# Backward 32x32 products on eight tiles of TensorE, in two PSUM banks, with a new order of heads

## The chip, the cores and the metric

One core of one Trainium2 chip runs the whole program: TensorE (PE, with its weight loads as PEld), VectorE (DVE), ScalarE (ACT), GpSimd (POOL) and the queue of SyncE (SP), from which most transfers are issued. The metric is the device time of one execution in microseconds (us). A measurement is the median of several runs; the profile is one more execution, taken by the hardware profiler.

## What is computed

A forward pass and the gradients of all its inputs, in bf16. Sequence 2048, width 512, 32 heads of 128, 64 segments of 32 rows, and 8 memory rows that go from each segment to the next. Cut to what matters:

```python
for s in range(n_seg):                       # 64, one after the other
    h = concatenate([mem, x_s])              # 8 + 32 rows
    q, k, v = (einsum('td,dhe->hte', h, W) for W in (Wq, Wk, Wv))
    p = softmax(where(mask, q @ k.T * scale, -1e9))
    o = einsum('hte,hed->td', p @ v, Wo)
    mem = o[:M]; outs.append(o[M:])
out = x + attention(layernorm(x)) + mlp(layernorm(x))     # mlp: relu(.)**2
grads = vjp(out)(grad_out)                   # x, mem0, Wq, Wk, Wv, Wo, w1, b1, w2, b2
```

The backward runs through the segments from the last to the first; the gradient of a segment's 8 memory rows is added to the output gradient of the segment before it. For each head it needs dP = gO v', dS from dP and P, and then dV = P'gO, dK = dS'q, dQ = dS k: products that contract over 32 rows and give 32 rows of 128.

## The kernel before

It has four stages: the MLP with its own backward, the forward recurrence, the backward recurrence, and the weight gradients with the layernorm backward.

**Layout.** The 32 heads of a segment stand as [128, 8, 128]: partition 32j + r holds row r of one head of group j (j = 0 to 3), and i = 0 to 7 counts the heads of the group. Head number is 4i + j. Memory rows of four segments (a block) form one more such array, the L arrays.

**Order.** In the first three stages nothing is ordered by hand. Each operation is added to a `_Plan` (L40) with a cost, the keys that it reads and writes, and a priority; `_Plan.run` (L101) lists them by the longest path that hangs on each, places each on its engine by its own estimate, and emits all engines' instructions in that order. `_TURN` (L22) is what the plan charges for a change of the shape of TensorE's tiles: "d" (32x32), "w" (128x32) and "f" (full array). A PSUM bank is a key too: `Stage.bank` (L350) deals the banks of a kind out in turn when an operation is added, before the plan is made.

**Backward recurrence** (`chain`, L1300, once a segment): project the output gradient (ps_gO, `proj`, L415), evict to gN, transpose on TensorE (ps_gOT), product dP (L1313), softmax gradient on VectorE (L1165 to L1170) into dS (the tile maskA), two 32x32 transposes of it on VectorE. Then three parts (L1319) for t = 2, 1, 0, each: products by `diag` (L441) in two halves into ps_d, eviction to dN, 32x32 transposes on VectorE (`sq_T`, L395) to dT, and four groups of matmuls against the transposed weights (`dh_part`, L1174) that add up in ps_dRA. That is copied to R_A, the memory rows are taken from it by small matmuls (ps_gm), and a copy puts them into the gradient of the segment before (L1353).

**32x32 products.** `diag` puts the matmul of group j on the tile at (32j, 32j): four of the array's sixteen tiles. A half is four of the eight i in one bank, two terms each (rows of the segment, and its memory rows):

```python
nc.tensor.matmul(
    bk()[32 * j:32 * j + m, k * P:(k + 1) * P], lhsT=lf(j, i), rhs=rf(j, i),
    start=(k == 0 and x == 0), stop=(x == n - 1), tile_position=(32 * j, 32 * j),
    skip_group_check=True,
)
```

**Block work.** `l_pre` (L1192) and `l_post` (L1228) do the same for the L arrays once per four segments, with lower priority: gL, gLT, dPL, dqL (by `diag`), then dL (an own part on 32x32 tiles at L1258, and a part over four segments read back from memory, L1269), and ps_dRL. They fill TensorE where the chain waits.

**Banks of the backward** (L1155): five of kind c for gO, gOT, dP, the chain's products and gm; one r for ps_dRA; two f for the block work. While the weights are turned (`turn`, L363), `rings` (L1379) deal differently.

**Last stage** (from L1500, ordered by hand): sixteen rounds of 20 x 8 matmuls [128, 512] into all eight banks, evicted in turn by ScalarE and VectorE. The plan before it does the first four banks of six rows of round 0 early (pw0, L1424).

Of the kernel before, what the change touches and what calls it, by code (L numbers as in the profile page):

```python
# [17 lines left out]
P = 128  # L18


_HOP = 0.06
_TURN = 0.095  # L22
# [13 lines left out]
class _Op:  # L36
    __slots__ = ("idx", "cost", "fn", "prio", "deps", "users", "left", "done", "end", "eng", "lat", "shape", "lift")


class _Plan:  # L40
# [12 lines left out]
    def add(self, cost, fn, R=(), W=(), prio=1, lat=None, lift=0.0):  # L53
        o = _Op()
        o.lift = lift
# [7 lines left out]
        o.users = []  # L63
        deps = set()
# [36 lines left out]
    def run(self):  # L101
# [4 lines left out]
        for o in reversed(ops):  # L106
            c = min(o.cost.values())
            t = 0.0
            for u in o.users:
                same = o.cost.keys() == u.cost.keys() and "SP" not in o.cost  # L110
                t = max(t, rank[u.idx] + (0.0 if same else o.lat + _HOP))
            rank[o.idx] = c + t + o.lift
# [3 lines left out]
        seq = []  # L116
        while elig:
            cand = []
            for o in elig:
                best = None  # L120
                g = _HOP + (0.0 if o.prio == 0 else self.grace)
                for e, c in o.cost.items():
                    t = 0.0
                    for d in o.deps:
                        t = max(t, d.end if d.eng == e and e != "SP" else d.end + d.lat + g)
                    s = max(t, free.get(e, 0.0) + (_TURN if o.shape not in (None, shape) else 0.0))
                    if best is None or s + c < best[0]:
                        best = (s + c, s, e, c)
# [32 lines left out]
            o.done = True  # L161
            elig.remove(o)
# [11 lines left out]
class _Bank:  # L174


    def __init__(self, pool, key, shape, dt, name):
        self.pool, self.key, self.shape, self.dt, self.name = pool, key, shape, dt, name
        self.t = None

    def __call__(self):
        if self.t is None:
            self.t = self.pool.tile(self.shape, self.dt, name=self.name, tag="%s%d" % self.key)
        return self.t
# [3 lines left out]
def kernel(  # L188
# [152 lines left out]
    class Stage:  # L341


        def __init__(self, plan, pools):
            self.plan = plan
            self.pools = pools
            self.cnt = {}
            self.rings = {}

        def bank(self, kind, shape, dt, name):  # L350
            ring = self.rings.get(kind) or [(kind, x) for x in range(self.pools[kind][1])]
            key = ring[self.cnt.get(kind, 0) % len(ring)]
            self.cnt[kind] = self.cnt.get(kind, 0) + 1
            return _Bank(self.pools[key[0]][0], key, shape, dt, name)
# [8 lines left out]
        def turn(self, kind, nm, reg, key, okey, g0=0, g1=DC * NI // 2):  # L363

            for g in range(g0, g1):
                dc, i0 = g % DC, 2 * (g // DC)
                blk = reg[:, dc, i0 * JQ * P:(i0 + 2) * JQ * P]
                bk = self.bank(kind, [P, 8, P], BF16, "ps_" + nm)

                def tr(e, blk=blk, bk=bk):  # L370
                    src = blk.rearrange("p (i m c) -> p i c m", i=2, c=JQ)
                    for i in range(2):
                        for c in range(JQ):
                            transpose_to(bk()[:, JQ * i + c, :], src[:, i, c, :])
                self.plan.add(pe(0.46, "f"), tr, [key] if g > g0 else [], [bk.key] + ([] if g > g0 else [key]), 1)
                self.evict(lambda blk=blk: blk, bk,
                           lambda bk=bk: bk()[:].rearrange("p k d -> p (k d)"), [(okey, g)], 1, {"DVE": 0.7, "ACT": 1.0})

        def turn_o(self, kind, nm, reg, key, okey, lift=0.0):

            for g in range(2 * NI):
# [8 lines left out]
                self.plan.add(pe(0.46, "f"), tr, [key] if g else [], [bk.key] + ([] if g else [key]), 1, lift=lift)  # L390
# [12 lines left out]
        def evict(self, out_f, bk, in_f, W, prio, cost, R=()):  # L403
            self.plan.add(cost, lambda e: ev({"DVE": "v", "ACT": "s"}[e], out_f(), in_f()),
                          [bk.key] + list(R), W, prio)

        def proj(self, kind, nm, win, wkeys, Wt, col0, dst, prio):
            for half in range(2):
                bk = self.bank(kind, [P, 512], F32, "ps_" + nm)
                for dq in range(2):  # L410
# [8 lines left out]
                    self.plan.add(pe(0.435, "w"), mm, wkeys, [bk.key], prio)  # L419
# [3 lines left out]
        def to_T(self, kind, nm, src, skeys, out_f, okeys, prio):  # L423
            for half in range(2):
# [5 lines left out]
                self.plan.add(pe(0.225, "f"), tr, [skeys[half]], [bk.key], prio)  # L430
# [3 lines left out]
        def to_T_plain(self, kind, nm, src, sk, dst, dk, prio):  # L434
# [4 lines left out]
                      [(dk, 0), (dk, 1)], prio)  # L439

        def diag(self, kind, nm, terms, rkeys, dst, prio, by=None):  # L441
            n = len(terms)
            for half in range(2):
# [12 lines left out]
                self.plan.add(pe(0.23 * n, "d"), mm, rkeys(half), [bk.key], prio)  # L456
                if by:
# [10 lines left out]
                    self.plan.add({"DVE": 0.70, "ACT": 0.92}, sc, [bk.key, by[0]], [(dst[0], half)], prio)  # L468
# [17 lines left out]
    def wf(t):  # L486
        w = Wqkv[t].rearrange("p c (i j e) -> p c i j e", i=NI, j=JQ)
        return lambda dc, c0: w[:, dc, c0 % HW // P:c0 % HW // P + 4, c0 // HW, :]
# [5 lines left out]
    def wtf(t, h):  # L494
# [28 lines left out]
    with tc.tile_pool(name="p0", bufs=1) as p0, \  # L523
# [41 lines left out]
        sg = Stage(plan, {"h": (pp, 4), "B": (pp, 4)})  # L565
# [12 lines left out]
        def ln(g):  # L578
# [24 lines left out]
            for k in range(2):  # L603
# [3 lines left out]
                A(pe(0.3, "f"), tr, [("xnN", w, k)], [bk.key])  # L607
            A({"DVE": 0.7}, lambda e: V.tensor_copy(xT[g % 2], bk()[:]), [bk.key], [("xT", g % 2)])
# [4 lines left out]
        def mlp_a(g):  # L613
            z = g % 2
            for fc in range(FC):
# [3 lines left out]
                for x, (Wt, wk, In, ik) in enumerate(((W1, ("W1", fc // 8), xT[z], ("xT", z)), (W2T, ("W2T", fc // 2), gTb[z], ("gT", z)))):  # L619
# [4 lines left out]
                    A({"PE": 0.44}, mm, [wk, ik], [bk.key] + ([("tick", g, fc)] if x else []))  # L624
                A({"ACT": 0.36}, lambda e, r=r, fc=fc, bk=bk: nc.scalar.activation(
                    r[:], bk()[:, 0, :], ACT.Relu, bias=b1T[:, fc:fc + 1], scale=1.0), [bk.key, "b1T"], [rk])
# [4 lines left out]
                    accum_out=gb1p[:, fc, g:g + 1]), [bk.key, rk], [("gh", z, fc), ("gb1p", fc, g)])  # L631
# [5 lines left out]
        def mlp_b(g):  # L637
            z, y3 = g % 2, g % 3
            for rc in range(2):
# [5 lines left out]
                A({"PE": 0.22}, b2m, ["b2r"], [bB.key])  # L645
# [924 lines left out]
```

## Time and profile before

| | us |
|---|---|
| median of 3 runs (3017.47 to 3035.89) | 3026.65 |
| span of the profiled execution | 3018.8 |
| TensorE busy | 2761.1 (91%) |
| VectorE busy | 1551.3 (51%) |
| ScalarE busy | 967.4 (32%) |
| forward recurrence, about | 230 to 1240 |
| backward recurrence, about | 1302 to 2440 |
| last stage, about | 2470 to 3019 |

Costliest groups in the backward by line: L1181 (ps_dRA) 382.5 us busy, L399 (sq_T to dT) 255.6, and each of the six terms of L451 on ps_d 67.6 to 74.3 (the six overlap; together L451 is busy 236.9 us from 1302 to 2422).

How to read it: a matmul's row gives its own length, filling and draining included, so that rows of neighbours overlap; the busy time of a group is the union of its rows. "128*32 128x512" is a matmul on 128 rows and 32 columns of the array whose moving operand has 512 columns. The chain of waits is followed back from the last instruction of the span or of a window: at each step to what released it.

### The profile page before, as it was taken

The page shows a single profiled execution, that of the slowest core. Times are in us where ns is not written, and L with a number is a line of the kernel's source. Part 1 is how long each engine was busy: PE and PEld are TensorE (multiplying, and loading weights), DVE is VectorE, ACT ScalarE, POOL GpSimd, SP SyncE. Part 2 cuts the span into 40 slices and gives each one's busy share as a digit, 9 for nine tenths or more (in the row PEclk, how much of TensorE's full clock was granted, in tenths as well). Part 3 has the DMA queues.
Part 4 walks back from the last instruction along what each step waited for, and adds up shares of the span by engine and source line. Part 5 has one row for each costly group of instructions (what it writes and reads, how often), then busy time and mean ns, then how long its engine had stood idle before and what let it go on. Part 6 is the DMA issues. An engine that isn't in the chain of part 4 may idle for free.

```text
span 3018.8 us, 132985 instructions
## 1 busy us (share of the span) xinstructions
PE 2761.1 (91%) x59680; PEld 1575.5 (52%) x59680; DVE 1551.3 (51%) x3367; ACT 967.4 (32%) x2013; POOL 372.8 (12%) x640
## 2 busy tenths in 40 slices
PE   8998899999999999888888888888889889999998
PEld 6664555555555555655454545454555444444444
DVE  5544555555555655666555555565556522232322
ACT  4324444444454444333333333333333310000000
POOL 1111111111111111100000000000000002111111
PEclk9999999999999999899999999999999999999999
DMA  6648655556555666457777877777777689788861
GB/s 202 221 141 227 166 170 168 162 159 172 167 166 162 174 182 179 135 162 197 196 208 197 211 215 208 202 204 207 204 215 205 193 292 311 232 262 271 248 182 42
DMA packets 543946, 590.15 MB, mean 195 GB/s; under 512 B 230342, under 2 KB 344183, under 8 KB 541199
## 3 DMA queue, kind: packets, MB, share of 16 engines
q1 hardware_dynamic: 527934, 527.05, 61.2%
q0 software_dynamic: 15440, 54.61, 5.4%
q8 instruction: 466, 7.63, 1.1%
q14 instruction: 106, 0.86, 0.1%
HBM read 283.32 MB, written 262.68 MB: 181 GB/s over the span
## 4 chain that ended last, share of the span: by engine, by line
PE 64%; issue 11%; DMA 10%; DVE 9%; SPq 2%; ACT 2%; POOL 1%; DVEq 0%; ACTq 0%; POOLq 0%
PE ps_gw L1517 11%; PE ps_dRA L1181 7%; PE ps_d L451 6%; PE ps_q L415 4%; PE ps_k L415 3%; PE ps_RA L863 3%; PE ps_h L622 3%; PE ps_gO L415 3%; PE ps_dw L1073 2%; PE ps_v L415 2%; PE ps_dRL L1181 2%; PE ps_B L650 2%; SPq L361 2%; PE ps_gxb L650 2%; DMA dLN<-S_GNL 1%
## 5 line engine op out<-in xcount | busy, mean ns | idle before, releaser
L1181 PE MATMUL ps_dRA<-WA,dT 128*32 128x512 bf16 x6144 | 382.5, 388 | 13.9 <-issue 10.2
L1517 PE MATMUL ps_gw<-WA,WB 128*128 128x512 bf16 x1536 | 332.3, 379 | 0.6 <-DVE gwo L316 0.6
L415 PEld LDWEIGHTS <-PA 128*32 128x32 bf16 x8192 | 204.9, 98 | 239.2 <-DVE PA L1011 27.0
L399 DVE STREAM_TRANSPOSE dT<-dN 128x512 bf16<-128x512 bf16 x384 | 255.6, 692 | 104.9 <-ACT dN L318 103.4
L1517 PEld LDWEIGHTS <-WB 128*128 128x128 bf16 x1896 | 185.4, 98 | 225.0 <-issue 1.7
L318 ACT CAST dN<-ps_d 128x512 bf16<-128x512 f32 x357 | 199.2, 588 | 287.5 <-PE ps_d L451 270.1
L1181 PEld LDWEIGHTS <-dT 128*32 128x32 bf16 x6144 | 158.5, 98 | 175.7 <-issue 34.4
L316 DVE CAST gwo<-ps_gw 128x512 bf16<-128x512 f32 x64 | 39.7, 683 | 401.7 <-PE ps_gw L1517 268.2
L318 ACT CAST gwo<-ps_gw 128x512 bf16<-128x512 f32 x64 | 32.9, 599 | 515.4 <-PE ps_gw L1517 357.9
L1291 POOL COPY bVT<-VR 128x1024 bf16<-128x1024 bf16 x64 | 66.7, 1043 | 965.9 <-PE ps_dP L1313 917.7
L415 PE MATMUL ps_q<-WA,PA 128*32 128x512 bf16 x2048 | 159.3, 387 | 8.4 <-DVE PA L1011 8.3
L316 DVE CAST kN<-ps_k 128x512 bf16<-128x512 f32 x120 | 83.0, 691 | 160.4 <-PE ps_k L415 158.7
L451 PEld LDWEIGHTS <-PB 32*32 32x32 bf16 x8192 | 119.1, 92 | 79.3 <-issue 45.9
L415 PE MATMUL ps_k<-WA,PA 128*32 128x512 bf16 x2048 | 158.0, 385 | 0.0
L415 PE MATMUL ps_gO<-WB,PA 128*32 128x512 bf16 x2048 | 138.3, 414 | 16.8 <-DVE PA L1353 15.3
L863 PE MATMUL ps_RA<-WB,OT 128*32 128x256 bf16 x4096 | 128.3, 275 | 14.6 <-DVE OT L399 10.5
L318 ACT CAST qN<-ps_q 128x512 bf16<-128x512 f32 x124 | 72.6, 586 | 198.8 <-PE ps_q L415 183.0
L1073 PE MATMUL ps_dw<-sx,anT 128*128 128x512 bf16 x448 | 123.7, 384 | 9.3 <-DMA sx<-in_grad_out_dram 4.7
L415 PE MATMUL ps_v<-WA,PA 128*32 128x512 bf16 x2048 | 129.3, 380 | 0.0
L863 PEld LDWEIGHTS <-OT 128*32 128x32 bf16 x4096 | 103.9, 97 | 39.1 <-DVE OT L399 30.6
L844 POOL TENSOR_TENSOR P<-P,rsA 128x320 bf16<-128x320 bf16 x64 | 46.2, 722 | 534.3 <-DVE rsA L839 228.1
L1181 PE MATMUL ps_dRL<-WA,LT 128*32 128x512 bf16 x1536 | 108.9, 387 | 2.3 <-issue 1.2
(307 smaller groups left out, 4920.1 us busy)
## 6 DMA issues: line engine op xcount, KB each, us to landing
S_GN<-dN SPq DMA_DIRECT2D x192, 256.0 KB
WA<-S_GN SPq DMA_DIRECT2D x160, 256.0 KB
S_Q<-qN SPq DMA_DIRECT2D x64, 256.0 KB
S_K<-kN SPq DMA_DIRECT2D x64, 256.0 KB
S_V<-vN SPq DMA_DIRECT2D x64, 256.0 KB
S_ON<-oN SPq DMA_DIRECT2D x64, 256.0 KB
bqN<-S_Q SPq DMA_DIRECT2D x64, 256.0 KB
bkN<-S_K SPq DMA_DIRECT2D x64, 256.0 KB
```

Of the source, the lines that this page charges most:

```text
L316: nc.vector.tensor_copy(out, in_)
L318: nc.scalar.copy(out, in_)
L399: self.plan.add({"DVE": 0.70}, lambda e, x=x: nc.vector.transpose(dst[:, x, :, :], src[:, x, :].rearrange("p i (a c) -> p i c a", c=JQ)), ...
L415: nc.tensor.matmul(bk()[32 * j:32 * (j + 1), :], lhsT=win(dc), rhs=Wt(dc, c0), start=(dc == 0), stop=(dc == DC - 1), tile_position=(0, 32 ...
L451: nc.tensor.matmul(bk()[32 * j:32 * j + m, k * P:(k + 1) * P], lhsT=lf(j, i), rhs=rf(j, i), start=(k == 0 and x == 0), stop=(x == n - 1), ...
L622: nc.tensor.matmul(bk()[:, x, :], lhsT=Wt[:, dc, fc * P:(fc + 1) * P], rhs=In[:, dc, :], start=(dc == 0), stop=(dc == DC - 1), skip_group_ ...
L650: nc.tensor.matmul(bk()[:], lhsT=src[z][:, fc, rc * P:(rc + 1) * P], rhs=Wt[:, fc, :], start=(fc == 0 and first), stop=(fc == FC - 1))
L863: nc.tensor.matmul(bk()[32 * c:32 * (c + 1), :], lhsT=OTt[:, i, j, :], rhs=Wo[:, JQ * i + j, dh * DH:(dh + 1) * DH], start=(i == 0 and j < ...
L1073: nc.tensor.matmul(bks[x]()[:], lhsT=anT[x][:, c, :], rhs=sx[z][:], start=(c == 0), stop=(c == TC - 1))
L1181: nc.tensor.matmul(bk()[32 * j:32 * (j + 1), :], lhsT=XT[:, i, j, :], rhs=wtf(t, JQ * i + j), start=(first and i == 0), stop=(last and i = ...
L1291: A({"POOL": 1.0}, lambda e: nc.gpsimd.tensor_copy(VT[:, :, :, M:KA].rearrange("p i j r -> p (i j) r"), VR[:].rearrange("p i j r -> p (i j ...
L1517: nc.tensor.matmul(bks[n]()[:], lhsT=HNc[:, rc, dc * P:(dc + 1) * P], rhs=gns[y][:, hf * 512:(hf + 1) * 512], start=(y == 0), stop=(y == N ...
```

## The change

It does three things.

1. **Heads dealt anew.** Head number is now 16 (i // 4) + 4 j + i % 4. The weights of q, k, v keep their place in memory, and the views of them change (`wf`, `wtf`, `turn`, the load of Wo, the writes of out_3 to out_6).
2. **Eight tiles.** In the backward, `cross` takes the place of `diag`. A half takes the groups j = 2 half and 2 half + 1 with all their i. The matmul of (j, i) goes to the tile at (32j, 32c), c = i % 4, so its result is at partition 32c; the two j of a half go to two banks, of which 256 columns each are used. Results stand as if i and j had changed their roles, and so `dh_part` asks `wtf` for another head. The forward's `diag` stays.
3. **Banks from the scheduler.** A `_Bank` of the backward has no key until the plan places its first operation; then it takes the free bank of its kind that came free earliest (`slots`). The kinds: c (at most 3), f (at most 1) and w (at most 3) share three banks, r has one, d two pairs, and t (turning the weights) uses r and the pairs. `l_post`'s own part and its other part follow each other in one pair. Three early banks, not four, serve the last stage, and they wait for gNat.

`ACCP` and `LIFT` are new parameters of the plan; both are zero.

```diff
-        sg = Stage(plan, {"c": (pc, 5), "r": (pc, 1), "f": (pc, 2)})
+        S3 = [("c", x) for x in range(3)]
+        sg = Stage(plan, pc, {"c": (3, S3), "f": (1, S3), "w": (3, S3), "r": (1, [("r", 0)]), "d": (2, [("d", 0), ("d", 1)]),
+                              "t": (3, [("r", 0), ("d", 0), ("d", 1)])})
...
+        def slots(o):
+            got = []
+            for w in o.banks:
+                if w.key is None:
+                    n, ways = w.group.ways[w.kind]
+                    if used.get(w.kind, 0) + sum(x[3].kind == w.kind for x in got) >= n:
+                        return None
+                    taken = [x[2] for x in got]
+                    can = [(loose.get(k, 0.0), x, k, w) for x, k in enumerate(ways)
+                           if loose.get(k, 0.0) is not None and k not in taken]
+                    if not can:
+                        return None
+                    got.append(min(can, key=lambda x: x[:2]))
+            return got
...
+        def cross(self, nm, terms, rkeys, dst, prio, lift=0.0):
+
+            n = len(terms)
+            for half in range(2):
+                bk = self.bank("d", [P, 2, 512], F32, "ps_" + nm)
+
+                def mm(e, half=half, bk=bk):
+                    self.cross_mm(bk, half, terms, True)
+                self.plan.add(pe(0.115 * n, "d"), mm, rkeys(half), [bk, (dst[0], half)], prio, lift=lift)
+                self.cross_evict(half, bk, dst, prio)
+
+        def cross_mm(self, bk, half, terms, first):
+            for s_ in range(2):
+                for x, (lf, rf, m) in enumerate(terms):
+                    for y in range(2):
+                        j = 2 * half + y
+                        for c in range(JQ):
+                            i = JQ * s_ + c
+                            nc.tensor.matmul(
+                                bk()[32 * c:32 * c + m, y, s_ * P:(s_ + 1) * P], lhsT=lf(j, i), rhs=rf(j, i),
+                                start=(first and s_ == 0 and x == 0), stop=(x == len(terms) - 1),
+                                tile_position=(32 * j, 32 * c), skip_group_check=True,
+                            )
+
+        def cross_evict(self, half, bk, dst, prio):
+            self.evict(lambda: dst[1][:, 4 * half:4 * half + 4, :].rearrange("p (y s) e -> p y (s e)", y=2), bk,
+                       lambda: bk()[:, :, 0:2 * P], [(dst[0], half)], prio, EV_F)
...
     def wf(t):
-        w = Wqkv[t].rearrange("p c (i j e) -> p c i j e", i=NI, j=JQ)
-        return lambda dc, c0: w[:, dc, c0 % HW // P:c0 % HW // P + 4, c0 // HW, :]
+        w = Wqkv[t].rearrange("p c (s j f) -> p c s j f", s=2, j=JQ)
+        return lambda dc, c0: w[:, dc, c0 % HW // 512, c0 // HW, :]
...
-    def wtf(t, h):
+    def wtf(t, i, q):
+        h = 16 * (i % 2) + JQ * (i // 2) + q
         return Wqkv[t][:, :, h * P:(h + 1) * P]
...
-                sg.diag("c", "d%d" % t, terms, rk, ("dN%d" % t, dN[t]), 0)
+                sg.cross("d%d" % t, terms, rk, ("dN%d" % t, dN[t]), 0, LIFT[t])
...
-                    A(pe(0.24, "d"), own, lk, [bks[half].key])
+                    A(pe(0.12, "d"), own_mm, lk + rk, [bk, ("dLN", half)])
...
-        pw0 = [sg.bank("c", [P, 512], F32, "ps_gw") for _ in range(4)]
+        pw0 = [sg.bank("w", [P, 512], F32, "ps_gw") for _ in range(3)]
...
-            A(pe(0.87, "f"), mm0, [("gn", y), ("HN", RCS[y] // BPC)], [b.key for b in pw0])
+            A(pe(0.65, "f"), mm0, [("gn", y), ("HN", RCS[y] // BPC), "gNat"], pw0)
...
-                                             rhs=gns[y][:, hf * 512:(hf + 1) * 512],
+                                             rhs=gns[y].rearrange("p (j s e) -> p s j e", j=JQ, s=2)[:, hf],
```

## The prediction

> **What bounds the kernel now.** I read the stages first, then the backward stage by line, then its chain of waits, then single bursts. The busy time by stretch (length, then each engine's busy us with its instruction count, granted TensorE clock, DMA share, GB/s) sets the backward recurrence, 1302 to 2422 us, beside a stretch of the last stage:
>
> ```profile
> 1302.00:2422.00 1120.00, 976.70 (x30197) 567.13 (x30189) 649.24 (x1293) 358.53 (x664) 90.13 (x138) 0.96 0.74 203
> 2500.00:2900.00 400.00, 400.00 (x1855) 181.37 (x1854) 113.94 (x187) 22.59 (x44) 72.66 (x101) 1.00 0.83 260
> ```
>
> The view of tile ps_gm (duration shortest/median/longest in ns, first and last start in us) gives the period:
>
> ```profile
> L1353 DVE CAST PA<-ps_gm x63: 152/192/193, 1301.8 to 2422.3; 128x32 bf16<-128x32 f32 x63
> ```
>
> The copy that hands one segment's memory gradient to the next has 62 periods in 1120.5 us, so a backward segment takes 18.1 us. TensorE is busy for 976.7 of the 1120 (15.8 us of a segment), VectorE for 58%, ScalarE for 32%. TensorE's work bounds the stage, with about 2.3 us of waiting per segment on top. The chain of waits over part of a segment (start, us, what) says where the work stands:
>
> ```profile
> 1845.52 0.33 PE ps_gOT L312 x4
> 1845.85 0.56 PE ps_d L451 x32
> 1846.40 0.34 PE ps_gOT L312 x4
> ...
> 1847.11 0.70 DVE dT L399
> 1847.81 0.47 DVE btA L1165
> 1848.28 0.02 issue
> 1848.30 0.50 DVE brA L1167
> 1848.80 0.02 issue
> 1848.83 0.50 DVE btA L1168
> 1849.33 0.02 issue
> 1849.35 0.50 DVE maskA L1170
> 1849.85 0.04 issue
> 1849.89 1.07 PE ps_d L451 x64
> 1850.97 0.98 PE ps_dRA L1181 x16
> 1851.94 0.33 PE ps_gLT L312 x4
> 1852.27 1.03 PE ps_d L451 x64
> ```
>
> Before maskA (dS) is ready the end waits for VectorE's softmax gradient; after it, TensorE runs product after product. The 32x32 products (L451) are on the path there.
>
> **The change, part by part.** *The products.* Their matmuls start in fours; the timeline of one burst shows the beat:
>
> ```profile
> 1799.85 0.22 PE L451 MATMUL ps_d<-bkLN,PB 32*32 32x128 bf16 x4
> 1799.91 0.22 PE L451 MATMUL ps_d<-bkN,PB 32*32 32x128 bf16 x4
> 1799.96 0.22 PE L451 MATMUL ps_d<-bkLN,PB 32*32 32x128 bf16 x4
> ```
>
> Four each 0.055 us, 13.8 ns a matmul. The busy time of L451 in one whole burst agrees (1.07 us for 64, of which 0.22 is the last one's own: 0.85 / 63 = 13.5 ns). With eight tiles the same beat would carry eight, 6.8 ns each, if loads and matmuls can be issued so fast. No row has eight tiles. The nearest, also with a weight load for each matmul and short streams, are ps_dP and ps_dPL, here by tile:
>
> ```profile
> 1720.00:1720.60 0.60, 0.38 (x32) 1.00 0.40 147
> 1785.00:1785.80 0.80, 0.69 (x64) 1.00 0.94 329
> ```
>
> With 0.18 us for the last one (ps_dP's mean): 0.20 / 31 = 6.5 ns and 0.51 / 63 = 8.1 ns. So a pair costs 6.5 to 8.1 ns; I take 6.8, as ps_dP carries more columns than ps_dPL and is the faster. Counts: chain products 6 x 2048 = 12,288 (the groups of L451), dqL 2 x 512 (16 blocks of 64), dL's own part (L1258) 16 x 64: 14,336 matmuls. Saved on TensorE: 14,336 x (13.6 - 6.8) = 97 us (79 at 8.1, 102 at 6.5). The eviction still moves 128x512 (588 ns on ScalarE) and the transposes stay; they are no cheaper.
>
> [...]
>
> *Tile shapes.* In the chain of waits a burst of 64 takes 1.00 us until ps_dP starts (1863.60 to 1864.61) where sixteen beats are 0.88: changing between 32x32, 128x32 and full arrays costs about 0.1 us. From the first gL projection to the last gm, the instruction orders of the two programs change shape 655 times before and 766 after. 111 x 0.1 = 11 us lost; 0 if they fall into waits, 14 at 0.13.
>
> *What reaches the end.* Four of a segment's six halves (d1, d0) stand behind maskA, where TensorE is the path. Check the cover: from maskA VectorE needs 0.14 + 0.43 + 0.40 (copy and two transposes) and four dT transposes of 0.69 = 3.7 us before the last 16 dRA can start. TensorE reaches them now after 0.88 + 0.87 + 0.88 + 48 x 0.052 and three changes of shape = 5.4 us; after the change 4.5 us, still the later, so those 2/3 count in full. The t=2 halves fill the wait for gOT, dP and the softmax gradient: in segments with little other filler the time saved there turns into waiting on maskA (TensorE's weight loads already wait 23.8 us for it). I count half. Net of switches, 97 - 11 = 86: 57 + 14 = 71 us.
>
> *Banks.* Seven banks served gO, gOT, dP, gm, the products and the block work; now three serve the first four with block work in at most one of them, and two pairs serve all products. Mostly this costs nothing: gOT needs gO evicted in any case. But in one segment of four the new order puts d0's second half behind 64 dRA, and the last 16 dRA then wait for 0.18 + 0.59 + 0.69 plus a hop = 1.5 us, covered by 0.85 us of dL: 0.65 x 16 = 10 us (0 to 20). There dqL stands ahead of gOT and covers 0.45 us of gON's eviction, worth up to 7 us, which I leave out of the sum. L1258's own part now waits for xs and ys too, as does what follows it today; behind it stand 16 dRL or dRA, and the wait on ys (13.4 us in all) stays where it is.
>
> *Weights turned, forward, last stage.* The instruction order of the forward is the same on all engines up to the turning of the weights; its strided and contiguous operands change places, and both kinds run now (L415 reads runs of 128, 4 matmuls of 512 columns in 0.22 us; L1517 reads runs of 512, 1855 in 400 us, one each 0.216 us). No DMA is added, and the runs written to out_3 to out_5 stay 256 bytes. Six early rows start three banks, not four: 6 x 0.216 = 1.3 us later work. In the last stage a pair is free only when both its halves are evicted: 0 to 0.2 us at 15 changes, I take 2. Before the last stage TensorE waits 6.55 us for maskL (VectorE behind a DMA of out_2); the new order leaves that wait, with products no longer sharing its bank: -5 to +5, I take 0.
>
> Sum: 71 - 10 - 3 = **58 us off** the span. The span of the profiled execution, 3018.8, is 7.9 under the median and near the lowest run (3017.47); the runs lie 0.6% apart. I take the 58 from the median: **2968**.
>
> **Rivals.** (a) *The chain takes over*: VectorE and ScalarE set the pace behind maskA too, and only a fifth is kept. Gain 17 us: 3010. For it: 3.7 against 4.5 us is thin. Against: both engines have room on average. (b) *Eight tiles don't run at once*, 13.6 ns stays: +11 + 3 = 3041, the edge of no change. Against: loads in ps_dP are issued at 6.5 ns. (c) *Pairs of banks run short*, the slower side: each of the three products has one half that waits a whole eviction on ScalarE (0.59) while nothing else may be ordered in: 3 x 0.59 x 64 = 113 against 71 - 3 = 68: 3072. It decides from 68 / 64 = 1.1 us of such waits per segment. For it: the delayed half above. Against: dRA fills the time between d1 and d0. (d) *Loads of one row group line up behind its matmuls*, since now four in a row share their rows: a pair would cost like gOT's full-array ones (8 in 0.62 us, 0.22 of it the last: 57 ns): 14,336 x (57 - 13.6) = +620, 3650. Against: dRA's loads use all rows, under running matmuls of 0.39 us, and 16 take 0.98 us.
>
> [...]
>
> **Chances.** Forecast 0.70 (its own range is 2912 to 2995: from 102 kept whole with the 7 and the 5 above, to 32), (a) 0.10, (b) 0.06, (c) 0.12, (d) 0.02. Under 0.5% (15 us) a measurement of this kernel can't tell from no change. Faster: 0.70 and most of (a), 0.78; same 0.07; slower 0.15. The range runs from 2912 past (a) to 3030 (the run spread of 0.6% on 3010) and leaves out (b), (c) and (d), 0.20.
>
> **What would show it.** L451's successor: 64 matmuls in about 0.65 us, in eights. Busy TensorE in the backward down by about 86 and its period near 17.1 us. Right if TensorE's waits on maskA grow by less than 20 us; wrong if waits on ps_d's evictions appear on TensorE (c), or bursts stay at 13.6 ns (b). Forward and last stage should stand within 5 us.

## The result and the profile after

The changed kernel takes 3107.7 us (median of 4 runs, 3089.6 to 3126.7). Beside runs of the kernel before on the same chip (median 3025.1 us) its time is 1.0277 times as long, 95% interval 1.0229 to 1.0326. The forecast was 2968 us and a range up to 3030 us: wrong in sign.

Its profiled execution has a span of 3106.7 us against 3018.8. Four marks divide both: the first and the last copy of memory rows in the forward (ps_mem), and the first and the last copy of the memory gradient (ps_gm).

| us | before | after | difference |
|---|---|---|---|
| until the first ps_mem copy | 256.0 | 303.5 | +47.5 |
| forward, to the last ps_mem copy | 958.7 | 956.7 | -2.0 |
| turning of the weights, to the first ps_gm copy | 87.1 | 95.4 | +8.3 |
| backward, 62 periods | 1120.5 | 1144.9 | +24.4 |
| from there to the end | 596.5 | 606.1 | +9.6 |

More than half of the loss lies before the forward has begun. There the queues by transfer (packets, MB, share of the 16 engines) and the loads of Wo (count, KB each, median us from issue to landing), from 215 to 310 us, are in the kernel before

```profile
q0 software_dynamic: 1728, 6.29, 20.2%
WB<-in_A_Wo_dram POOLq DMA_DIRECT2D x8, 512.0 KB, 11.7
```

and after

```profile
q0 software_dynamic: 4704, 6.04, 70.5%
WB<-in_A_Wo_dram POOLq DMA_DIRECT2D x8, 512.0 KB, 39.8
```

About the same bytes take three and a half times the engines' time, in 2.7 times the packets. The median 512 KB load lands after 39.8 us, not 11.7. The view of waits from 215 to 320 us (total, times, longest) shows who stands behind them; in the kernel before the same wait came once, for 1.8 us:

```profile
PE ps_RA L932 <- DMA WB<-in_A_Wo_dram: 30.6, 3, 28.4
```

In the backward, the stretch view and the period after are

```profile
1356.00:2501.00 1145.00, 953.20 (x30144) 480.15 (x30140) 645.66 (x1278) 361.23 (x672) 89.85 (x138) 0.94 0.74 199
```

```profile
L1417 DVE CAST PA<-ps_gm x63: 150/192/193, 1355.6 to 2500.6; 128x32 bf16<-128x32 f32 x63
```

The trace has as many matmuls and loads as before (to 0.2%), and the stretch of 1120 us has become 1145 us although TensorE is busy 23 us less. The granted clock fell from 0.96 to 0.94. Eight tiles do run at once; the timeline of a burst (start, us) is

```profile
1938.70 0.25 PE L498 MATMUL ps_d<-bkN,PB 32*32 32x128 bf16 x8 [0.41 <-ACT dN L357]
1938.76 0.25 PE L498 MATMUL ps_d<-bkLN,PB 32*32 32x128 bf16 x8
```

Eight start every 0.055 us where four did. What becomes of the saved time shows in the chain of waits around that burst:

```profile
1937.62 0.43 PE ps_d L498 x32
1938.04 0.02 issue
1938.07 0.59 ACT dN L357
1938.66 0.04 issue
1938.70 0.41 PE ps_d L498 x32
1939.12 1.51 issue
1940.62 5.32 PE ps_dRA L1252 x64
```

Three things are to be read here. The second burst waits for the first to be evicted (0.59 us). Then TensorE stands for 1.51 us in which the profile shows nothing that it waits for ("issue"). And the 64 matmuls on ps_dRA behind it take 5.32 us; at the 0.052 us of the kernel before they would take 3.3. Three stretches of 3.41 us each, over the same place (PEclk is the third number from the end), tell why:

```profile
1934.75:1938.17 3.42, 2.60 (x95) 1.28 (x95) 3.35 (x9) 0.27 (x2) 1.07 (x2) 1.00 1.31 304
1938.17:1941.58 3.41, 1.49 (x66) 0.93 (x56) 1.97 (x4) 1.56 (x3) 0.00 (x0) 1.00 0.86 172
1941.58:1944.99 3.41, 3.41 (x40) 1.56 (x36) 1.30 (x2) 0.00 (x0) 0.00 (x0) 0.50 0.45 159
```

In the second stretch TensorE is idle for 1.92 us of 3.41, and the third runs at half clock. The last section counts how often the one came with the other.

So a length of the backward can be taken apart: TensorE's busy time, less half of what falls into half-clock stretches, is taken as its work at full clock; that half is lost to the clock; the rest is idle, either "issue" or a wait for something named (which of the two a wait is put down to can shift these two columns by some 2 us). The half is read from ps_dRA in the changed kernel's backward: its matmuls start in fours, 0.206 us apart (median) at full clock and 0.411 at half.

| us | backward | work at full clock | lost to half clock | idle, issue | idle, other |
|---|---|---|---|---|---|
| before | 1120.5 | 939 | 39 | 62 | 80 |
| after | 1144.9 | 885 | 69 | 94 | 97 |

The change took 54 us of work off TensorE, and 79 us came back: 30 of clock, 32 of issue, 17 of named waits.

Among the named waits one grew by more than the whole 17. TensorE's waits in the backward, before and after, have these lines:

```profile
PE ps_dRA L1181 <- DVE dT L399: 2.1, 2, 1.4
PE ps_dRA L1252 <- DVE dT L438: 31.4, 31, 2.6
```

Twelve of the 31 are over 1 us and make up 24 us. In each of them VectorE runs two or three steps of the softmax gradient before the transpose that TensorE waits for.

What is behind "issue" shows in the instruction queue q8, whose packets fit TensorE's instructions in number, over the whole backward (the same line before and after):

```profile
q8 instruction: 236, 3.87, 1.5%
```

236 packets of 16 KB for the 60,284 matmuls and loads of the changed kernel are 255 a packet. All 85 issue waits of over 0.3 us in this backward end 1.1 to 1.7 us after a packet of q8 has ended, and so do all 56 in the kernel before; of moments picked at random 12% do, of the 116 other waits of the changed kernel 7. (The wait at 1939.12 ends 1.35 us after one.) Their place is as regular. If TensorE's instructions are counted through from the first one in the trace, all 85 of these waits end at place 41 or 42 of a group of 256 (counted from 0), and all 56 in the kernel before at place 193 or 194; the other waits lie evenly over the 256 places. The author reads the two counts together: TensorE stands there until a next packet, of 256 instructions, has come. No run changed the packets to test that.

In both kernels no two such packets start less than 3.25 us apart; the packet that ends an issue wait starts 4.9 us (median) behind the one before it. If a packet holds 128 pairs of load and matmul, that is 25 ns a pair at the least distance, an estimate from these two numbers. A pair took 13.6 ns in a burst before and takes 6.5 to 8.5 now. Whether 3.25 us is a limit or only the least that came up, no run shows.

The 56 waits come to 59 us before, the 85 to 91 us after.

### The profile page after: what moved, and what is told of

Its sections match the earlier page's. It is cut to its first block, busy times and chain, and to the rows that moved or that the text cites. A ratio compares the mean times of both kernels' runs of the same rounds, so it can differ in the third digit from the quotient of the medians.

```text
span 3106.7 us, 132903 instructions
## 1 busy us (share of the span) xinstructions
PE 2728.8 (88%) x59515; PEld 1486.2 (48%) x59680; DVE 1554.5 (50%) x3360; ACT 969.8 (31%) x2020; POOL 373.5 (12%) x640
## 4 chain that ended last, share of the span: by engine, by line
PE 47%; issue 15%; DVE 7%; DMA 7%; ACT 3%; SPq 1%; POOL 1%; DVEq 0%; ACTq 0%; POOLq 0%
PE ps_dRA L1252 9%; PE ps_gw L1582 8%; PE ps_d L498 4%; PE ps_gO L454 3%; PE ps_q L454 3%; PE ps_RA L932 2%; PE ps_k L454 2%; PE ps_dRL L1252 2%; DMA ys<-S_PL 2%; PE ps_v L454 1%; PE ps_dw L1142 1%; SPq L401 1%; PE ps_gOT L351 1%; DMA WA<-S_GN 1%; PE ps_o L518 1%
## 5 line engine op out<-in xcount | busy, mean ns | idle before, releaser
L1252 PE MATMUL ps_dRA<-WA,dT 128*32 128x512 bf16 x6144 | 429.6, 419 | 58.4 <-DVE dT L438 32.2
L1252 PEld LDWEIGHTS <-dT 128*32 128x32 bf16 x6144 | 160.5, 104 | 257.1 <-issue 91.3
L454 PE MATMUL ps_gO<-WB,PA 128*32 128x512 bf16 x2048 | 124.8, 384 | 12.7 <-DVE PA L1417 11.7
L1252 PE MATMUL ps_dRL<-WA,LT 128*32 128x512 bf16 x1536 | 117.2, 399 | 6.8 <-issue 6.8
L1142 PE MATMUL ps_dw<-sx,anT 128*128 128x512 bf16 x319 | 102.2, 385 | 12.5 <-DMA sx<-S_XN 5.0
L355 DVE CAST gON<-ps_gO 128x512 bf16<-128x512 f32 x64 | 44.2, 691 | 132.0 <-PE ps_gO L454 129.9
## 6 DMA issues: line engine op xcount, KB each, us to landing
S_GN<-dN SPq DMA_DIRECT2D x192, 256.0 KB
WA<-S_GN SPq DMA_DIRECT2D x160, 256.0 KB
S_Q<-qN SPq DMA_DIRECT2D x64, 256.0 KB
S_K<-kN SPq DMA_DIRECT2D x64, 256.0 KB
S_V<-vN SPq DMA_DIRECT2D x64, 256.0 KB
S_ON<-oN SPq DMA_DIRECT2D x64, 256.0 KB
bqN<-S_Q SPq DMA_DIRECT2D x64, 256.0 KB
bkN<-S_K SPq DMA_DIRECT2D x64, 256.0 KB
```

The lines of the kernel that those rows point to most:

```text
L355: nc.vector.tensor_copy(out, in_)
L454: nc.tensor.matmul(bk()[32 * j:32 * (j + 1), :], lhsT=win(dc), rhs=Wt(dc, c0), start=(dc == 0), stop=(dc == DC - 1), tile_position=(0, 32 ...
L1142: nc.tensor.matmul(bks[x]()[:], lhsT=anT[x][:, c, :], rhs=sx[z][:], start=(c == 0), stop=(c == TC - 1))
L1252: nc.tensor.matmul(bk()[32 * j:32 * (j + 1), :], lhsT=XT[:, i, j, :], rhs=wtf(t, i, j), start=(first and i == 0), stop=(last and i == NI - ...
```

## The experiments

Times are ratios to runs of the kernel before on the same chip; parts of the backward are as in the table above, from one profile each.

| run | ratio, 95% interval | first ps_mem | turning | backward | work | half clock | issue | other |
|---|---|---|---|---|---|---|---|---|
| e1_wo_by_head | 1.0146 (1.0119 to 1.0174) | 263.0 | 96.1 | 1137.4 | 879 | 68 | 92 | 98 |
| e2_wo_strided_on_sp | 1.0237 (1.0203 to 1.0272) | 284.8 | 96.0 | 1145.7 | 883 | 66 | 103 | 95 |
| e3_four_tiles | 1.0179 (1.0141 to 1.0218) | 262.6 | 98.7 | 1164.9 | 902 | 88 | 84 | 90 |
| e4_given_banks | 1.0136 (1.0105 to 1.0167) | 256.1 | 87.3 | 1150.4 | 930 | 61 | 56 | 104 |
| e5_few_banks | 1.0180 (1.0155 to 1.0204) | 257.1 | 98.4 | 1164.2 | 950 | 39 | 77 | 98 |
| e6_banks_in_turn | 1.0693 (1.0627 to 1.0759) | 264.3 | 90.7 | 1313.5 | | | | |
| e7_waits_only | 1.0234 (1.0181 to 1.0287) | 255.0 | 86.7 | 1190.1 | 934 | 69 | 56 | 131 |
| e8_turns_in_rank | 1.0894 (1.0834 to 1.0953) | 264.4 | 91.4 | 1366.0 | | | | |
| e9_turns_in_rank_four | 1.0148 (1.0090 to 1.0206) | 257.1 | 88.2 | 1179.3 | | | | |
| e10_other_order | 1.0079 (1.0055 to 1.0103) | 262.4 | 95.4 | 1113.1 | 865 | 71 | 102 | 75 |
| e11_any_two_banks | 1.0015 (0.9994 to 1.0035) | 262.1 | 86.0 | 1127.0 | 876 | 56 | 102 | 93 |
| e12_any_two_reordered | 1.0126 (1.0078 to 1.0175) | 261.7 | 86.0 | 1137.1 | 869 | 87 | 106 | 75 |
| e13_any_two_lift1 | 0.9989 (0.9963 to 1.0015) | 262.2 | 86.4 | 1117.8 | 885 | 68 | 77 | 88 |
| e14_wo_two_queues | 1.0001 (0.9978 to 1.0024) | 265.9 | 85.9 | 1117.0 | 884 | 69 | 80 | 85 |
| e15_any_two_four_tiles | 1.0048 (1.0019 to 1.0078) | 262.6 | 86.7 | 1127.4 | 900 | 56 | 83 | 89 |
| e16_any_two_cost | 1.0054 (1.0029 to 1.0080) | 262.6 | 85.2 | 1121.7 | 873 | 69 | 104 | 76 |
| e17_half_products | 0.9714 (0.9679 to 0.9749) | 254.7 | 86.7 | 1030.8 | 854 | 37 | 17 | 123 |
| e18_longer_softmax | 1.0019 (0.9997 to 1.0040) | 255.2 | 87.9 | 1119.7 | 940 | 26 | 54 | 100 |

### The load of Wo

e1_wo_by_head:

```diff
-    sg.dma(lambda i=i: Wo[:, JQ * i:JQ * (i + 1), :].rearrange("p c d -> p (c d)"),
-           lambda i=i: A_Wo.rearrange("(s j x) (a c) d -> s x j a (c d)", s=2, j=JQ, c=JQ)[i // JQ, i % JQ],
+    for j in range(JQ):
+        sg.dma(lambda i=i, j=j: Wo[32 * j:32 * (j + 1), JQ * i:JQ * (i + 1), :].rearrange("p c d -> p (c d)"),
+               lambda i=i, j=j: A_Wo[16 * (i // JQ) + JQ * j + i % JQ].rearrange("(a c) d -> a (c d)", c=JQ),
...
-           lat=8.0, cost=0.6, eng="POOL")
+               lat=8.0, cost=0.15, eng="POOL")
```

> The changed kernel with one edit: each of the eight loads of Wo is split into four, one per head, so that each takes 32 whole rows of 4096 B that lie one after the other; what lands where is the same. Theory W (the load whose source strides over heads is slow and holds up the forward recurrence): the first copy of memory rows in the forward comes back from 303.5 to about 256 us, and the time falls from 3108 by about 47 us to 3060. Rival W0 (the late start has another cause, and the load only ends last): less than 10 us, 3098 or more. Half-way (the packets are slower because the destination or the order of the heads is, not the stride): 3075 to 3095.

The first copy came at 263.0, and the ratio fell from 1.0277 to 1.0146, some 40 us. In its queues, same view and stretch:

```profile
q0 software_dynamic: 2064, 6.16, 27.0%
WB<-in_A_Wo_dram POOLq DMA_DIRECT2D x32, 128.0 KB, 7.6
```

The load's form is shown as the cause of 40.5 of the 47.5 us.

e2_wo_strided_on_sp, from the changed kernel:

```diff
-                   lat=8.0, cost=0.6, eng="POOL")
+                   lat=8.0, cost=0.6, eng="SP")
```

> The changed kernel with the eight strided loads of Wo issued from SyncE's queue instead of GpSimd's; source, destination and pattern as in the change. Theory W1 (the stride over heads is slow on GpSimd's software queue only): the first copy of memory rows in the forward is back near 256 to 265 us and the ratio near that of e1_wo_by_head, 1.015. Rival W2 (such a source is slow from any queue): the first copy at 295 us or later, ratio 1.025 or more.

Neither held: 284.8. A packet of 4096 B takes 170 ns on average here, against 651 ns in GpSimd's queue from 215 to 310 us in the changed kernel (199 ns in the kernel before), so the slow packets belong to this pattern on that queue. But the eight loads still last from 224.8 to 272.5 us, as the DMA share (second number from the end) shows between 240 and 260 us:

```profile
240.00:260.00 20.00, 3.74 (x84) 1.84 (x76) 2.16 (x6) 2.60 (x4) 0.00 (x0) 0.69 0.26 104
```

0.26 of 16 engines is the busy time of four. In the trace's packets, four of 4096 B are in flight for 37.8 of those 47.7 us.

The new source begins with a dimension of 4, and four packets in flight are what e2 shows; that the one sets the other was not shown. Why a packet takes 651 ns when GpSimd issues the same pattern, in the changed kernel with 14 or more in flight for 49 of 73 us, no run shows either.

e14_wo_two_queues, from e13 (below):

```diff
-lat=8.0, cost=0.15, eng="POOL")
+lat=8.0, cost=0.15, eng=("POOL", "ACT")[j % 2])
```

> e13 with half of the 32 loads of Wo issued by ScalarE instead of GpSimd. The first copy of memory rows in the forward, 262 us in e13 and 256 in the kernel before, comes back to 256 to 259 if the issue of 32 loads on one queue (0.49 us each, 16 us in all) is what is left of the load's cost; no change if it is something else; later by 5 us or more if the issues hold up ScalarE's own work.

265.9 instead of 262.2, ratio 1.0001: the issue of 32 loads is not what is left. The last 6 us stay open.

### Tiles, banks and order

e3_four_tiles, from e1:

```diff
-for s_ in range(2):
-    for x, (lf, rf, m) in enumerate(terms):
-        for y in range(2):
-            j = 2 * half + y
+for y in range(2):
+    j = 2 * half + y
+    for s_ in range(2):
+        for x, (lf, rf, m) in enumerate(terms):
             for c in range(JQ):
```

> The kernel of e1_wo_by_head with the loops of the eight-tile products turned so that the two head groups of a half follow each other: four tiles run at a time, as in the kernel before, in the same banks, with the same plan. It is to be held against e1_wo_by_head. Theory P (the products' time on TensorE is no longer on the path: behind them the chain waits for evictions and transposes): within 15 us of e1_wo_by_head, bursts of 64 at 13 ns a matmul instead of 8.5. Rival B (eight tiles do save what was worked out for them, about 70 us, and banks take more than that away): 50 us or more above e1_wo_by_head.

The ratios lie 0.33% apart, 10 us, and the medians 15, which is at the edge of theory P's 15; the intervals of the two ratios just overlap, and the profiles' backward grew by 27. Rival B's 50 us are out. But the beat is not the one that was expected: these four tiles share one group of rows, and a burst of 64 runs at 10.4 ns a matmul, not 13. TensorE's work grew by 23 us only, so the run undoes a part of the gain and not the whole.

e4_given_banks and e5_few_banks are the kernel before with the changed kernel's `_Plan` and `_Bank`. A product (`diag`) also waits for the array that it is evicted to, as in `cross`; in e4 gL and gLT do so too, which the changed kernel does not have:

```diff
-sg = Stage(plan, {"c": (pc, 5), "r": (pc, 1), "f": (pc, 2)})
+e4: {"c": (5, C5), "f": (2, F2), "w": (4, C5[:4]), "r": ..., "t": (4, [c4, f1, c2, c3])}
+e5: {"c": (3, S3), "f": (1, S3), "w": (3, S3), "r": ..., "d": (2, [d0, d1]), "t": (3, [r0, d0, d1])}
-A(pe(0.24, "d"), own, lk, [bks[half].key])
+A(pe(0.24, "d"), own, lk + rk, [bks[half], ("dLN", half)])     # both; halves one after the other
```

> The kernel before with its products, its heads and its bank counts (five c, one r, two f), but the banks are given by the scheduler as in the changed kernel. To keep it from running out of banks, an operation that takes a bank of the block work or of the products also waits until the array that it will be evicted to is free. Theory P and rival B both leave this within 10 us of the kernel before (3025). Rival S (the giving itself costs, since the waits for a bank no longer count in the plan's longest paths): 25 us or more slower, 3050 or above.

> The kernel before with its four-tile products and its heads, but with the changed kernel's banks: three shared by c and f (f one at a time), one r, two at a time for all products of 32x32 (one bank each where the changed kernel has two). Theory P: the shortage costs little, backward up to 25 us longer than the 1120 us of before, time 3025 to 3050. Rival B: the shortage costs about what eight tiles were to save and more, 70 to 100 us: 3095 to 3125. Rival S: as e4_given_banks, within 10 us of it.

e4 is 41 us slower, e5 54 us. Rival S seemed right, though it wanted the two within 10 us. But added waits came in with the giving, and e7_waits_only was their control. It is the kernel before, its banks dealt in turn, with all the waits of e4: the products, gL, gLT and dL's own part (the last line of the diff) wait for their arrays, that part also for xs and ys, the halves of dL follow each other, and the last stage waits for gNat.

> A control for e4_given_banks: the kernel before, its banks dealt in turn, with the added waits of e4_given_banks alone (a product, gL, gLT and dL wait for the array that they are evicted to; both halves of dL after each other; the end waits for gNat). Theory S: within 10 us of before, since the giving made e4_given_banks 40 us slower. Rival K (those added waits did it): 25 us or more slower, ratio 1.009 or more.

Rival K: the waits alone cost 70 us in the backward, the giving takes some 40 of them back, and theory S falls. The view of waits of e7 says where (total, times, longest):

```profile
PE ps_d L451 <- DVE maskA L1170: 71.4, 33, 3.4
```

In half of the segments the products wait 2.2 us for the softmax gradient. In the kernel before those waits on maskA were 23.8 us on the weight loads, 84.8 in e7. What is missing is work to fill them with: over the 64 stretches from the start of btA to the end of maskA, TensorE was busy for 107 us before and for 55 in e7. There ps_dRA fell from 49.5 to 22.8 us, gL and dqL together from 25.2 to 3.0, ps_dRL from 30.3 to 18.6; dL's own part, 0.7 us before, rose to 5.2. So several fillers moved, and dL's own part was hardly one of them. Which of the added waits moved them was not run one by one.

e6_banks_in_turn (from e1), and e8_turns_in_rank and e9_turns_in_rank_four (one edit, from e1 and from e4) asked the same of the scheduler:

```diff
e6, e1's banks dealt when an operation is added:
-"c": (3, S3), "f": (1, S3), "w": (3, S3), "d": (2, [d0, d1]), "t": (3, [r0, d0, d1])
+"c": (None, [c0, c1]), "f": (None, [c2]), "w": (None, S3), "d": (None, [d0, d1]), "t": (None, [r0, d0, d1])
e8 and e9, in the longest paths (vusers: the operations that wait for o's bank if banks went in turn):
-for u in o.users:
+for u in o.users + o.vusers:
```

> The kernel of e1_wo_by_head (eight tiles, Wo by head) with the banks dealt in turn when an operation is added, as in the kernel before: two banks for c, one for f, one r, two pairs d. To be held against e1_wo_by_head (1.0146 of before). Theory S (the giving by the scheduler costs some 30 us of the backward, as e4_given_banks had it): the backward falls from 1137 to 1105 to 1115 us, the time to about 1.005 of before. Rival B2 (fixed turns waste banks where there are so few; two c banks in turn wait more than three shared ones): equal to e1_wo_by_head or slower, 1.015 or more.

> The kernel of e1_wo_by_head, banks given by the scheduler, but the plan's longest paths are worked out as if the banks went in turn (c two, f one, the pairs two), so that an operation that holds a bank counts for who comes next in turn. Theory S1 (the giving costs because a wait for a bank is missing in the longest paths, so that the plan lists operations in a worse order): 20 to 35 us below e1_wo_by_head, ratio 1.003 to 1.008. Rival S2 (it costs by the choice of the bank or the time at which it is taken): within 8 us of e1_wo_by_head.

> The same edit on e4_given_banks (the products, heads and bank counts of before, banks given by the scheduler), with a turn of five c and two f banks in the longest paths. S1: the 40 us that e4_given_banks lost come back but for 10, ratio below 1.004, and the waits of TensorE on maskA, 70 us in that run, fall below 25. S2: ratio 1.010 or more, waits on maskA as they were.

Theories S and S1 fell: 1.0693, 1.0894, and 1.0148 beside 1.0136. e6 went the way of rival B2 and e9 the way of S2 (71 us of waits on maskA where e4 has 70); that e8 would come out 7% above e1 neither theory had. With banks this few, fixed turns (two banks for c, one for f) end 7% behind the kernel before, the giving (e1) 1.5%; bank turns in the plan's ranks are not what is missing.

e10_other_order and e11_any_two_banks, both from e1:

```diff
e10:
-KEEP = 2.0; ACCP = 0.0; LIFT = (0.0, 0.0, 0.0)
+KEEP = 2.5; ACCP = 0.2; LIFT = (0.0, 0.0, 1.0)
e11:
-"c": (3, S3), "f": (1, S3), "w": (3, S3), "d": (2, [d0, d1]), "t": (3, [r0, d0, d1])
+"c": (3, S7), "f": (2, S7), "w": (3, S7[0:3]), "d": (4, S7), "t": (4, S7[3:7])
-bk = self.bank("d", [P, 2, 512], F32, "ps_" + nm)
+bk = [self.bank("d", [P, 512], F32, "ps_" + nm) for _ in range(2)]     # each evicted by itself
```

> The kernel of e1_wo_by_head with three parameters of the plan changed and nothing else (ACCP 0 to 0.2, LIFT of t = 2 from 0 to 1.0, KEEP 2.0 to 2.5): same instructions, same tiles, same counts of banks, another order. Theory O (the backward did not fall because of the order that the plan found, in which TensorE stands before dT; the banks allow a better one): the backward falls from 1137 by 15 to 40 us, ratio to before 1.002 to 1.010. Rival B (two pairs are too few, whatever the order): the backward within 8 us of 1137, ratio 1.012 to 1.017.

> The kernel of e1_wo_by_head with freer banks: a half's two banks are any two of seven (c, f and d share the seven; at most three c, two f instead of one, two halves as before), each bank is evicted by itself (twice as many evictions, each of half the size) and is free again after it. Rival B: the waits on dT and the idle time of TensorE fall, the backward falls by 30 us or more below 1137, ratio to before below 1.004; the turning before the backward also gets 10 us shorter, as four banks serve it. Theory O: the backward moves as its order happens to come out, in either direction, and the waits on dT stay above 25 us.

Another order alone takes 24 us off the backward, at unchanged banks: theory O. The waits for dT went (37 us in e1, 2 in e10), but waits on maskA came in their place (2 and 34). Freer banks take 10 off the backward, 10 off the turning and 8 off the end, 1.0015 in all. TensorE's waits for dT before ps_dRA fell from 37 to 20 us, those on maskA rose from 2 to 18, and its whole idle time grew from 190 to 195, so rival B's mechanism is not shown, only that the turning wants four banks. e12 and e13 joined both, from e11:

```diff
e12:
-pe(0.115 * n, "d"); "c": (3, S7); "d": (4, S7); KEEP = 2.0; ACCP = 0.0; LIFT = (0.0, 0.0, 0.0)
+pe(0.25 * n, "d"); "c": (4, S7); "d": (6, S7); KEEP = 2.5; ACCP = 0.3; LIFT = (0, 0, 1.0)
e13:
-KEEP = 2.0; ACCP = 0.0; LIFT = (0.0, 0.0, 0.0)
+KEEP = 2.5; ACCP = 0.2; LIFT = (0, 1.0, 0)
```

> e11_any_two_banks with the plan's cost of a product at what the trace shows for eight tiles (0.5 us for a half of two terms, where the change wrote 0.23), up to three halves at once, and ACCP 0.3, LIFT 1.0 for t = 2, KEEP 2.5. Both theories expect it at or below e10 and e11; if order and banks are what was missing, it is below the kernel before: ratio 0.985 to 0.998. If the loss lies with the half-clock stretches alone, which more waiting on a faster TensorE brings, it stays above 1.0.

> e11_any_two_banks with the plan's KEEP 2.5, ACCP 0.2 and LIFT 1.0 for t = 1: another order alone. If order and banks add up, as e10 (order, 24 us off the backward) and e11 (banks, 10 us off the backward and 10 off the turning) suggest, the backward comes to 1095 to 1115 us and the ratio to 0.990 to 0.998. If what is left is the waiting itself and its half-clock stretches, whatever the order, the backward stays at 1113 to 1140 and the ratio at 0.998 or above.

e12, with the true cost of a product in the plan (and more halves at once, and other parameters), is slower than e11; e13 comes to 0.9989, no difference from the kernel before, which is what its second case expected.

e16_any_two_cost was a third order, from e11: a product's cost at 0.08 a term, KEEP 0.5, ACCP 0.3, four c banks. It expected a backward anywhere from 1100 to 1137 and found 1121.7, at a ratio of 1.0054. One of its eleven outputs is wrong by 6%, for a reason that stays open, so it is no kernel to use. The orders tried move the backward by up to 24 us, and none of these kernels is faster than the one before.

e15_any_two_four_tiles is e11 with e3's loops:

> e11_any_two_banks with the products' loops turned as in e3_four_tiles: four tiles at a time, same plan, same banks. It says what eight tiles are worth where banks are freer. If banks were what kept the gain of eight tiles away, it is 45 us or more above e11 (backward above 1172); if evictions, transposes and the half-clock stretches keep it away, it is 10 to 30 us above, as e3 was above e1 (27 us in the backward).

It expected 10 to 30 us above e11 if not the banks but other things keep the gain away. The ratios lie 10 us apart, with intervals that overlap. In the profiles the backward has the same length, as the two stretches show, e11 first:

```profile
1306.00:2433.00 1127.00, 930.80 (x30242) 478.25 (x30240) 701.01 (x1439) 363.25 (x984) 89.88 (x138) 0.95 0.74 202
```

```profile
1310.00:2437.00 1127.00, 954.58 (x30239) 500.72 (x30236) 704.52 (x1437) 364.33 (x983) 90.03 (x138) 0.95 0.73 202
```

24 us more busy time, and no microsecond of length in these two executions. The difference stands mostly in the column "issue": 83 us with four tiles, 102 with eight. What faster products save here, TensorE spends for the most part in issue waits.

### Was TensorE's work the bound before?

Two edits of the kernel before, with the plan's costs as they were:

```diff
e17, in diag:
-for x, (lf, rf, m) in enumerate(terms):
+for x, (lf, rf, m) in enumerate(terms[:1] if nm in ("d0", "d1", "d2") else terms):
e18, in smax_bwd:
-V.tensor_reduce(rr[:], st[:], axis=AX.X, op=ALU.add)
+for _ in range(2 if sfx == "A" else 1):
+    V.tensor_reduce(rr[:], st[:], axis=AX.X, op=ALU.add)
```

> The kernel before, with the second terms (the memory rows) left out of the chain's three products d2, d1, d0: 6144 of 12,288 matmuls fewer, at 13.6 ns some 84 us less for TensorE, with nothing else in the plan changed. The gradients lack that part. Theory T (TensorE's work bounds a segment of the backward, as the prediction had it): the backward falls by 55 us or more, below 1066. Theory C (a segment waits for a chain through VectorE's and ScalarE's steps, and TensorE's work fills its gaps): it falls by less than 30, to 1092 to 1120, and the idle time of TensorE grows by about what its work loses.

> The kernel before, with the sum over a row in the chain's softmax gradient done twice on VectorE (0.50 us more per segment, 32 us in all; TensorE's work and the plan's order as they are; the result is the same). Theory C: the whole step is on the path, so the backward grows by 25 to 40 us, to 1145 to 1160. Theory T: TensorE has work to do meanwhile, so the backward grows by less than 12 us.

```profile
1301.00:2331.00 1030.00, 889.30 (x24224) 474.37 (x24220) 637.83 (x1293) 355.68 (x664) 89.86 (x138) 0.96 0.81 220
```

```profile
1304.00:2423.00 1119.00, 964.72 (x30192) 562.73 (x30177) 678.81 (x1355) 358.30 (x664) 89.85 (x138) 0.98 0.74 203
```

Theory T, clearly: 85 us less work make the backward 90 us shorter, with the idle time as it was (142 and 140 us), and 32 us more of softmax cost nothing (12 us more idle time, 13 less lost to the clock). And a detail that separates two ways of saving: e17 drops instructions, 24,224 matmuls instead of 30,197, and its issue waits fall from 62 to 17 us. Eight tiles drop none. But what left the issue waits of e17, 45 us, came back as named waits (80 to 123 us), so an issue wait that goes is not a microsecond won. These waits end at two neighbouring places of 256 in e17 too (15 of 15 at place 41 or 42), on which the reading that TensorE stands for instructions rests. What fewer such waits alone would be worth had no run.

## Why the prediction was wrong

**What bounds the kernel.** Right. TensorE's work is the bound of the kernel before (e17, e18).

**The beat (97 us).** The mechanism was right and the size near: 6.5 ns in bursts of 32, as read from ps_dP, and 8.5 in bursts of 64, just above the upper end of 8.1. Rivals (b) and (d) are out. The work at full clock fell by 54 us net, where 86 were worked out; between e5 and e1, which have the same limits on banks, it fell by 71.

**What reaches the end (71 us).** This step failed. It took a saved microsecond of work for a saved microsecond of time wherever TensorE was later than VectorE. Two costs that came with the faster bursts were missing: issue waits (+32 us) and half-clock stretches (+30 us). The cover check of 4.5 against 3.7 us looked at VectorE behind maskA alone. Ahead of maskA VectorE does hold TensorE up: the waits of ps_dRA for dT grew by 29 us, and the twelve long ones, 24 us, lie in the part t = 2, whose saved time was counted at half. From e5 to e1, 71 us less work bring 27 us: 29 went to the clock and 15 to issue.

**Banks (10 us).** The delayed d0 half was seen rightly, but the term was mis-sized. From before to e5, with four tiles and the change's limits, the backward grows by 44 us: 11 of work, 15 of issue and 18 of named waits. Of added waits the step has only that of L1258's own part, which it leaves at nothing; that each product of the chain now waits for its array as well, as `cross` has it, is not in the step. e7 measured 70 us in the backward for these two kinds of wait together with those of gL and gLT, which the changed kernel does not have. What each of them costs, and how much they cost in the changed kernel, was not run.

**Forward and weights (0 us).** Failed, and by itself nearly as large as the whole forecast gain. "No DMA is added" was true, and the load's new source pattern was in the diff; only the operands of TensorE were asked about their strides. e1 puts it at 40.5 of 47.5 us.

**Turning and last stage (3 us).** The turning grew by 8 us; its banks had been four (two for Wq), and became three that it shares with ps_dRA and the products (with four of seven, in e11, it takes 86.0). The end lies between 591 and 606 us in the runs here, without a pattern that an edit explains.

**Signs.** TensorE's waits on maskA grew by less than 20 us, as the forecast wanted (they fell from 23.8 to 10.0), but in name only: the waits for dT came in their place. Busy TensorE fell by 23 us, not 86, the period is 18.5 us, not 17.1, and the end moved by 9.6 us where 5 were allowed. Waits on the eviction of dN appeared as rival (c) wanted (6.1 us before ps_d, 15 times), and decided little. Rival (c)'s time was nearest, 3072; its mechanism was a small part.

## What to carry to other kernels

A change that makes instructions faster without making them fewer is checked for what the issue waits do: here they went from 62 to 94 us. Read a diff of layouts at every transfer, and not only at the engines' operands: here the source pattern of the loads of Wo was worth 40.5 us. Where a scheduler orders the work, an added wait of a filler operation is an edit of the order, and its price is measured, not read off the operation. A wait that shrinks is looked for under other names before it counts as gone.

## What was not expected of the hardware

Issue waits of over 0.3 us in the backward ended 1.1 to 1.7 us after a 16 KB packet of the instruction queue q8: 85 of 85 after, 56 of 56 before, 15 of 15 in e17. In each of the three kernels they fell on two neighbouring places of a group of 256 instructions, counted through the whole program.

In the backward of both kernels the half clock came in stretches of one to three times 3.41 us, and mostly behind a stretch of 3.41 us with much idle time in sum. With 1.6 us idle or more the next stretch ran at half clock in 21 of 23 cases before and 17 of 19 after; with less than 0.8 us in 1 of 256 and 9 of 232. One long gap was not needed: in three of the 23 no single gap reached 1.0 us, and all three were followed by half clock. Between 1.2 and 1.6 us it was 2 of 18 before and 16 of 30 after, so the sum alone did not decide there.

The changed kernel's load of Wo, whose source begins with a dimension of 4, had four packets in flight for 37.8 of 47.7 us from SyncE's queue, at 170 ns each, and took 651 ns a packet from GpSimd's.
